# Retention and a rational feed-forward layer: masks made on chip, the sign of twelve weight tiles on GpSimd, and a written-out order of all steps

## The chip, the cores and the metric

The kernel runs on one core of a Trainium2 chip. A core has five engines with a queue of instructions each: TensorE (PE, with PEld for its weight loads), VectorE (DVE), ScalarE (ACT), GpSimd (POOL) and SyncE (SP), which here only issues the DMA transfers. Each engine works through its own queue in order and waits at semaphores for the others. The metric is the device time of one launch in microseconds (us); less is better.

## What is computed

The reference first makes a retention layer with decay `gamma` per head, over 4 batches, 8 heads, 768 positions of 64 dimensions, and then a feed-forward layer whose activation is a quotient of polynomials:

```python
for t in range(S):
    state = gamma[None, :, None, None] * state + np.einsum('bhd,bhe->bhde', k[:, :, t], v[:, :, t])
    y[:, :, t] = scale * np.einsum('bhd,bhde->bhe', q[:, :, t], state)
...
h = x @ w_in
h2 = h * h
h3 = h2 * h
P = a[0] + a[1] * h + a[2] * h2 + a[3] * h3
Q = 1.0 + np.abs(b[0]) * np.abs(h) + np.abs(b[1]) * h2
g = P / (Q + 1e-06)
return (g @ w_out).astype(np.float32)
```

x holds the 3072 tokens of 512 values that the retention gives; w_in is 512 x 2048 and w_out 2048 x 512. Both weights arrive as float64.

## The kernel before

**Retention.** The 768 positions of a batch are cut into 6 chunks of 128. The first chunk of each of the four batches has no state behind it (`first_chunk`): scores S = k q on PE (tile pa), a product with a mask of decays M on DVE (tile aT), values R = aT v on PE (tile px), and then XH and XL, which split the result into a rounded part xh (ACT) and the rest xl (DVE), since every large product is made of three fp32r products of such parts. The masks of the first chunks (tile first, two halves) and of the later ones (mask_sb), and the output decays xdec_sb, are inputs that are loaded. `first_states` makes the states after the first chunks (pk on PE, state on DVE) from k that POOL has scaled (V). The later chunks come in pairs of batches (`later_chunks`): S in two bursts (pa, then pk), M, U(E), which adds the old state to half of pk and gives mid, R (px), a product with xdec_sb, XH and XL. Lc4 is the first such pair, Lc6 the second.

**Feed-forward.** The 3072 tokens are 6 blocks n of 512, the 2048 hidden units 16 tiles f of 128; a slot is one pair (n, f), numbered 0 to 95 in the order of `TURNS`: block 0 with f 0 to 7, block 1 with f 0 to 7, then both with 8 to 15, then blocks 2 to 5. IN(k) is the 12 matmuls of slot k into ph (line 825), OUT(k) the 12 into po (line 844), which takes four PSUM banks b4 to b7. Between them ACT makes A1 = |h| (tile q), A2 (tile s, on POOL for 16 slots), A3 (tile p); POOL makes P1 = q s; DVE makes D1 (two instructions); ACT A4 (reciprocal square root and square, into ph); DVE D2 (three instructions, lines 934 to 936; the first is called N below); ACT A6 = gh, the rounded g; POOL P2 = gl, the rest. ph has two banks, b0 and b1, so IN(k+2) waits for D2(k).

**Weights.** `decode` turns one float64 tile of 128 x 512, as two 32-bit words each (raw), into fp32r parts: ACT makes t from the top byte of the low word (low, line 784), ACT u from the high word without its sign (high, line 788), DVE joins both with the sign in two instructions (join, lines 794 and 797), ACT rounds (split, line 803), POOL takes the rest (line 806). The tile for (m, f) is w_in for m = 0 and w_out for m = 1. There are 32.

**Order.** Every piece of work is a `Step` with engines, costs, predecessors and a rank. `Plan.order` runs through a model of the engines while the kernel is built and always emits the step that can begin first, by rank among those close together; tables of ranks (`RANKS`, `OFFSETS`, `NUDGES`, `LOADS`) tip it. Where the model sees a gap on PE of over 700 ns, it puts matmuls of zeros there (`zeros_for`). Loads are issued by SP in the order of the plan; buffers come from pools with the depths in `BUFS`, and a load waits at SP until its buffer is free.

```python
            nc.vector.scalar_tensor_tensor(
                u_, u_, 3, t_, ALU.logical_shift_left, ALU.bitwise_or
            )
            nc.vector.scalar_tensor_tensor(
                t_, cell["raw"][:, :, 1], 0x80000000, u_, ALU.bitwise_and, ALU.bitwise_or
            )
```

Of the kernel before, what the change touches and what calls it, by code (L numbers as in the profile page):

```python
# [10 lines left out]
U32 = mybir.dt.uint32  # L11
U8 = mybir.dt.uint8
# [8 lines left out]
LANES = 8  # L21
WAKE = 60
ARRAY = 163
BEGIN, ISSUE, LATENCY, LANDED, RATE = 350, 470, 1850, 560, 408
STALLS = (3300, 1400), (13000, 1300)
LEAVE, ENTER = 92, 111
COLD = 1200, 1700
FULL, LATE = 66000, 2000


def zeros_for(gap):

    return min(12, int(gap / FILL)) if gap > 700 else 0

# [18 lines left out]
class Plan:  # L53
# [4 lines left out]
    def __init__(self, depths, banks):  # L58
        self.depths, self.turns = depths, {}
        self.held = {b: None for b in banks}  # L60
        self.steps, self.free, self.landings, self.claims = [], {"SP": BEGIN}, [], []
        self.stalls = list(STALLS)
        self.pipe, self.tiled, self.begun = 0, False, False

    def step(
        self, engines, cost, run, after=(), rank=0.0, takes=(), uses=(), tiled=False, kind=None
    ):
        rank += OFFSETS.get(kind, 0.0) + NUDGES.get(len(self.steps), 0.0)
        if not isinstance(cost, dict):
            cost = {e: cost for e in engines}  # L70
        x = Step(engines, cost, run, after, rank, list(takes), list(uses), tiled)
        for b in x.uses:
            b.users += 1
        self.steps.append(x)
        return x

    def freed(self, buffer):
        if buffer is None:
            return 0
        return None if buffer.users else buffer.end  # L80

    def banks_of(self, buffer, x):

        best = None
        for option in buffer.options():
            ends = [self.freed(self.held[b]) for b in option]
            if None in ends or best and max(ends) >= best[0]:
                continue
            begin = max(x.known, *ends) + HOLD
            if any(y is not x and y.rank < x.rank and y.known < begin and not wanted.isdisjoint(option)  # L90
                   for y, wanted in self.claims):
                continue
            best = max(ends), option
        return best

    def ready(self, x):
        t = x.known
        for b in x.takes:
            if b.options:
                found = self.banks_of(b, x)  # L100
                end = found and found[0]
            else:
                turns = self.turns.setdefault(b.pool, [])
                n = self.depths[b.pool]
                end = self.freed(turns[-n]) if len(turns) >= n else 0
            if end is None:
                return None
            t = max(t, end + WAKE if end else 0)
        return t

    def commit(self, x, engine, t):
        for b in x.takes:
            if b.options:
                b.banks = self.banks_of(b, x)[1]
                for name in b.banks:
                    self.held[name] = b
            else:
                self.turns[b.pool].append(b)
        busy, done = x.cost[engine] if isinstance(x.cost[engine], tuple) else (x.cost[engine],) * 2
        if engine == "PE" and x.tiled != self.tiled:  # L120
            self.tiled = x.tiled
            extra = LEAVE if x.tiled else ENTER
            busy, done = busy + extra, done + extra
# [1337 lines left out]
```

## Time and profile before

| | |
|---|---|
| time, median of 3 runs | 609.01 us (608.49 to 609.05) |
| profiled execution | 608.67 us, of which the span in the trace is 607.0 |
| PE busy | 596.5 us, 98% of the span |
| DVE, ACT, POOL busy | 442.4, 430.0, 330.4 us |
| DMA | 59.43 MB, mean 98 GB/s |

A row of the timeline gives the start, the length, the engine, the line of the kernel, the operation, the tiles written and read, how many instructions were merged into the row, and in brackets how long the engine stood idle before it and what ended that. Matmuls overlap each other, so the next row on PE can begin before the end of the last. A chain row gives a start, a length and the work.

### The profile page before, as it was taken

What the parts mean: (1) busy time and instruction counts of PE and PEld (TensorE: products, weight loads), DVE (VectorE), ACT (ScalarE), POOL (GpSimd) and SP (SyncE); (2) the same over time, 40 slices, a digit from 0 to 9 for tenths busy, and PEclk for the clock granted to TensorE, in tenths of its full rate; (3) what the DMA queues carried; (4) which work ended last, traced back from release to release, by engine and by line L of the source; (5) the groups of instructions that cost most, each with busy time, mean ns of one, the idle gap of its engine ahead of it and who ended that gap; (6) DMA issues with size and microseconds to landing.
All of it is one profiled execution on the core that took longest, in us unless ns stands there. A gap on an engine that the chain in (4) does not pass through costs nothing.

```text
span 607.0 us, 12921 instructions
## 1 busy us (share of the span) xinstructions
PE 596.5 (98%) x5230; PEld 486.5 (80%) x5230; DVE 442.4 (73%) x665; ACT 430.0 (71%) x699; POOL 330.4 (54%) x276
## 2 busy tenths in 40 slices
PE   7998999999999999999999999999999999999997
PEld 5766888888888888878888888888888888888885
DVE  3899999898778778676666766567777666666664
ACT  3899899999756574666666775577675766767663
POOL 0789598796756554646445554454463345544452
PEclk9999999999999999999999999999999999999999
DMA  8999901011314263404005101400240000100001
GB/s 317 409 409 413 374 0 70 1 52 36 105 70 130 75 217 85 159 19 157 2 1 176 69 1 26 151 0 6 83 137 22 1 1 1 70 0 1 0 2 69
DMA packets 30411, 59.43 MB, mean 98 GB/s; under 512 B 3216, under 2 KB 8592, under 8 KB 30352
## 3 DMA queue, kind: packets, MB, share of 16 engines
q1 hardware_dynamic: 30352, 58.61, 26.7%
q8 instruction: 41, 0.67, 0.4%
q14 instruction: 18, 0.15, 0.1%
HBM read 50.21 MB, written 8.39 MB: 97 GB/s over the span
## 4 chain that ended last, share of the span: by engine, by line
PE 90%; DVE 0%; ACT 0%; issue 0%
PE po L844 43%; PE ph L825 41%; PE px L420 3%; PE pa L390 2%; PE pk L399 2%; DVE p L936 0%; DVE t L797 0%; DVE ph L935 0%; DVE q L934 0%; ACT o L991 0%
## 5 line engine op out<-in xcount | busy, mean ns | idle before, releaser
L907 POOL TENSOR_TENSOR q<-q,s 128x512 f32<-128x512 f32 x96 | 124.2, 1294 | 184.6 <-ACT s L896 172.6
L825 PE MATMUL ph<-xh,w 128*128 128x512 f32 (+2 forms) x776 | 208.4, 391 | 2.5 <-ACT w L803 1.5
L844 PE MATMUL po<-w,gh 128*128 128x512 f32 x768 | 199.6, 392 | 0.0
L825 PEld LDWEIGHTS ph<-xh,w 128*128 128x128 f32 x776 | 143.7, 188 | 33.8 <-ACT w L803 2.4
L844 PEld LDWEIGHTS po<-w,gh 128*128 128x128 f32 x768 | 143.1, 188 | 30.2
L934 DVE SCALAR_TENSOR_TENSOR q<-q,small,ph 128x512 f32<-128x512 f32 x96 | 71.6, 746 | 112.3 <-ACT ph L923 109.7
L946 POOL TENSOR_TENSOR gl<-p,gh 128x512 fp32r<-128x512 f32 x96 | 124.2, 1294 | 36.6 <-ACT gh L942 19.7
L922 ACT ACTIVATE s<-q,small 128x512 f32<-128x512 f32 x96 | 69.5, 724 | 64.8 <-POOL q L907 64.8
L844 PE MATMUL po<-w,gl 128*128 128x512 f32 x384 | 110.5, 390 | 0.0
L887 ACT ACTIVATE q<-ph 128x512 f32<-128x512 f32 x96 | 57.4, 598 | 69.6 <-PE ph L825 69.3
L825 PE MATMUL ph<-xl,w 128*128 128x512 f32 (+2 forms) x388 | 103.3, 388 | 0.0
L825 PEld LDWEIGHTS ph<-xl,w 128*128 128x128 f32 x388 | 72.6, 188 | 15.2
L844 PEld LDWEIGHTS po<-w,gl 128*128 128x128 f32 x384 | 72.0, 188 | 15.2 <-POOL gl L946 0.3
L902 ACT ACTIVATE p<-ph,small 128x512 f32<-128x512 f32 x96 | 74.5, 776 | 0.0
L916 DVE SCALAR_TENSOR_TENSOR p<-p,small,ph 128x512 f32<-128x512 f32 x96 | 71.7, 747 | 3.4
L915 DVE TENSOR_TENSOR p<-ph,p 128x512 f32<-128x512 f32 x96 | 65.8, 685 | 8.8 <-ACT p L902 8.4
L935 DVE SCALAR_TENSOR_TENSOR ph<-p,small,ph 128x512 f32<-128x512 f32 x96 | 71.9, 749 | 0.0
L936 DVE SCALAR_TENSOR_TENSOR p<-q,ph 128x512 f32<-128x512 f32 x96 | 65.9, 687 | 3.3
L942 ACT CAST gh<-p 128x512 fp32r<-128x512 f32 x96 | 59.1, 616 | 12.2 <-DVE p L936 12.0
L896 ACT ACTIVATE s<-q,small 128x512 f32<-128x512 f32 x80 | 65.0, 812 | 0.1
L923 ACT ACTIVATE ph<-s 128x512 f32<-128x512 f32 x96 | 57.8, 602 | 4.2 <-DVE p L916 0.9
L806 POOL TENSOR_TENSOR w<-t,w 128x512 fp32r<-128x512 f32 x32 | 41.4, 1296 | 22.3 <-DMA k<-in_k 14.8
(59 smaller groups left out, 416.6 us busy)
## 6 DMA issues: line engine op xcount, KB each, us to landing
v<-in_v SPq DMA_DIRECT2D x34, 256.0 KB, 4.9
raw<-in_w_in SPq DMA_DIRECT2D x16, 512.0 KB, 7.9
raw<-in_w_out SPq DMA_DIRECT2D x16, 512.0 KB, 8.5
qT<-in_qT SPq DMA_DIRECT2D x24, 256.0 KB, 4.6
kT<-in_kT SPq DMA_DIRECT2D x24, 256.0 KB, 4.6
k<-in_k SPq DMA_DIRECT2D x24, 256.0 KB, 4.1
out<-o SPq DMA_DIRECT2D x24, 256.0 KB, 2.3
q2T<-in_q2T SPq DMA_DIRECT2D x10, 256.0 KB, 4.6
```

The lines of the kernel that those rows point to most:

```text
L825: nc.tensor.matmul(cell["ph"][:, t0:t1], w[0, f][:, part, kt * P : (kt + 1) * P], x[:, kt, t0:t1], start=(i == 0), stop=(i == 3 * NP - 1),)
L844: nc.tensor.matmul(o_tiles[n][tt], g_[:, tt * P : (tt + 1) * P], w[1, f][:, part], start=(first and m == 0), stop=(last and m == 2),)
L896: nc.scalar.activation(cell["s"], cell["q"], AF.Identity, bias=babs[:, 0:1], scale=babs[:, 1:2])
L902: nc.scalar.activation(cell["p"], cell["ph"], AF.Identity, bias=par_sb[:, 2:3], scale=par_sb[:, 3:4])
L907: nc.gpsimd.tensor_mul(cell["q"], cell["q"], cell["s"])
L915: nc.vector.tensor_mul(p_, ph_, p_)
L916: nc.vector.scalar_tensor_tensor(ph_ if aside else p_, p_, par_sb[:, 1:2], ph_, ALU.add, ALU.mult)
L922: nc.scalar.activation(s_, cell["q"], AF.Abs_reciprocal_sqrt, bias=qcon[:, 0:1])
L934: nc.vector.scalar_tensor_tensor(q_, q_, qcon[:, 0:1], ph_, ALU.add, ALU.mult)
L935: nc.vector.scalar_tensor_tensor(ph_, p_, par_sb[:, 0:1], ph_, ALU.add, ALU.mult)
L936: nc.vector.scalar_tensor_tensor(p_, q_, 2.0, ph_, ALU.subtract, ALU.mult, reverse0=True)
L946: nc.gpsimd.tensor_sub(cell["gl"], cell["p"], cell["gh"].bitcast(F32))
```

## The change

**Masks.** The inputs mask0, mask1 and xdec are gone. One input of 204 columns, powers, is loaded third; it holds the first four powers of each block, the factors for doubling and a causal pattern. `grow` copies the first four columns and then doubles the width with one product each. DVE makes the first masks so (seven instructions), POOL makes xdec_sb (six) and mask_sb (one). The 816 columns live in the buffer of weight tile (1, 15), which is loaded after them.

**Sign.** For 12 weight tiles in the table POOL writes the sign from the top byte into the upper 16 bits of t; ACT's low then writes only the lower 16 bits, and the join on DVE is one instruction.

**A2.** POOL makes it for 25 slots instead of 16.

**Order.** The planner is gone: `ORDER` lists the 1767 steps, `BANKS` the PSUM banks, `ZEROS` the zero matmuls. D2 is now two steps, N and the rest, which may be apart. Code for an exact product of some slots is added, but its list (`EXACT`) is empty.

```diff
     def order(self, emit):
...
+        for i in ORDER:
+            x = self.steps[i]
+            for b in x.takes:
+                if b.options:
+                    b.banks = [f"b{j}" for j in BANKS[i]]
+            x.start = True
+            emit(x, x.engines[0], ZEROS.get(i, 0))
...
+    def grow(engine, to, first, by):
+
+
+        n, w = to.shape[1], 4
+        engine.tensor_copy(to[:, :, :4], first.rearrange("p (b t) -> p b t", t=4))
+        while w < to.shape[2]:
+            engine.tensor_mul(
+                to[:, :, w : 2 * w], to[:, :, :w], by[:, :n].unsqueeze(2).broadcast_to([P, n, w])
+            )
+            w, by = 2 * w, by[:, n:]
+
+    def first_masks(rank):
+
+
+        def run(_):
+            to, causal = lent["first"], lent["causal"]
+            grow(nc.vector, to.rearrange("p (b t) -> p b t", t=D), lent["first4"], lent["first_by"])
+            for r, blocks in ((0, slice(0, 3, 2)), (1, slice(0, 2))):
+                y = to[half(r)].rearrange("p (b x t) -> p b x t", x=3, t=D)[:, :, blocks]
+                by = causal[half(r)].unsqueeze(1).unsqueeze(1).broadcast_to([D, 4, 2, D])
+                nc.vector.tensor_mul(y, y, by)
+            for s in range(2):
+                masks[s] = to[:, s * 6 * D : (s + 1) * 6 * D]
...
+    def later_mask(_):
+        to = mask_sb.rearrange("p e h t -> p (e h) t")
+        by = lent["later"].unsqueeze(2).broadcast_to([P, 2 * NP, D])
+        nc.gpsimd.tensor_mul(to, by, lent["causal"].unsqueeze(1).broadcast_to([P, 2 * NP, D]))
+
+    def later_decay(_):
+        to = xdec_sb.rearrange("p r a t -> p (r a) t")
+        grow(nc.gpsimd, to, lent["decay4"], lent["decay_by"])
...
+        def sign(_):
+            cell["t"] = ff.tile([P, DM], U32, name="t", tag=t_tag, bufs=BUFS[t_tag])
+            byte = cell["raw"].rearrange("p m w -> p (m w)").bitcast(U8)[:, 7::8]
+            if aside:
+                nc.gpsimd.tensor_scalar(
+                    cell["t"].bitcast(U16)[:, 1::2], byte, 128.0, 32768.0, op0=ALU.is_ge, op1=ALU.mult
+                )
 
         def low(_):
-            cell["t"] = ff.tile([P, DM], U32, name="t", bufs=BUFS["t"])
             byte = cell["raw"].rearrange("p m w -> p (m w)").bitcast(U8)[:, 3::8]
-            nc.scalar.activation(cell["t"], byte, AF.Identity, bias=lcon[:, 0:1], scale=1.0 / 32)
+            to = cell["t"].bitcast(U16)[:, 0::2] if aside else cell["t"]
+            nc.scalar.activation(to, byte, AF.Identity, bias=lcon[:, 0:1], scale=1.0 / 32)
...
+            if aside:
+                nc.vector.scalar_tensor_tensor(
+                    t_, u_, 3, t_, ALU.logical_shift_left, ALU.bitwise_or
+                )
+                return
...
-        load_first(0, "s", -10 + 0.012)
-        load_first(1, "p", -10 + 0.014)
-        const_load("mask", mask_sb.rearrange("p e h t -> p (e h t)"), mask1, CONSTS)
-        const_load("xdec", xdec_sb, xdec, CONSTS)
+        load_powers(-11)
+        first_masks(-10)
+        for name, cost, run in (("mask", (1250, 1300), later_mask), ("xdec", (2300, 2400), later_decay)):
...
+    ("sign", (0, 0)): "POOL", ("sign", (0, 1)): "POOL", ("sign", (0, 4)): "POOL",
+    ("sign", (0, 6)): "POOL", ("sign", (0, 12)): "POOL", ("sign", (0, 14)): "POOL",
+    ("sign", (0, 15)): "POOL", ("sign", (1, 4)): "POOL", ("sign", (1, 5)): "POOL",
+    ("sign", (1, 6)): "POOL", ("sign", (1, 7)): "POOL", ("sign", (1, 8)): "POOL",
...
+ORDER = (
+    20, 19, 1, 58, 6, 7, 24, 2, 72, 32, 11, 59, 12, 8, 13, 60, 61, 26, 33, 73, 4, 21, 14, 74, 25,
```

What stands on DVE behind the products with xdec_sb of the pair Lc4, before. u<-u,t and t<-raw,u are a join, p<-ph,p and p<-p,small,ph are D1, xl is XL:

```order
L457 TENSOR_TENSOR px<-px,xdec_sb 128x512 x2
L794 SCALAR_TENSOR_TENSOR u<-u,t 128x512
L797 SCALAR_TENSOR_TENSOR t<-raw,u 128x512
L472 TENSOR_TENSOR xl<-px,xh 128x2x2x128 x2
L794 SCALAR_TENSOR_TENSOR u<-u,t 128x512
L797 SCALAR_TENSOR_TENSOR t<-raw,u 128x512
L915 TENSOR_TENSOR p<-ph,p 128x512
L916 SCALAR_TENSOR_TENSOR p<-p,small,ph 128x512
```

And in the changed kernel at the same place, where t<-u,t is a join of one instruction and q<-q,small,ph is N, the first instruction of D2:

```order
L317 TENSOR_TENSOR px<-px,xdec_sb 128x512 x2
L862 TENSOR_TENSOR p<-ph,p 128x512
L863 SCALAR_TENSOR_TENSOR p<-p,small,ph 128x512
L719 SCALAR_TENSOR_TENSOR t<-u,t 128x512 x2
L332 TENSOR_TENSOR xl<-px,xh 128x2x2x128
L664 TENSOR_TENSOR state<-pk,small 128x256 x2
L874 SCALAR_TENSOR_TENSOR q<-q,small,ph 128x512
L332 TENSOR_TENSOR xl<-px,xh 128x2x2x128
```

D1 of slot 2 moved ahead of the joins, the two joins here became one instruction each, and the second pair's state of the first chunks moved in.

What stands on POOL behind gl of slot 5, before (gl<-p,gh is P2, q<-q,s is P1, s<-q,small is A2, w<-t,w the rest of a weight tile):

```order
L946 TENSOR_TENSOR gl<-p,gh 128x512
L892 TENSOR_SCALAR s<-q,small 128x512
L907 TENSOR_TENSOR q<-q,s 128x512
L806 TENSOR_TENSOR w<-t,w 128x512
L946 TENSOR_TENSOR gl<-p,gh 128x512
L806 TENSOR_TENSOR w<-t,w 128x512
L892 TENSOR_SCALAR s<-q,small 128x512
```

And in the changed kernel from gl of slot 4 on, where t<-raw is a sign:

```order
L894 TENSOR_TENSOR gl<-p,gh 128x512
L701 TENSOR_SCALAR t<-raw 128x512 x2
L838 TENSOR_SCALAR s<-q,small 128x512
L735 TENSOR_TENSOR w<-t,w 128x512
L853 TENSOR_TENSOR q<-q,s 128x512
L701 TENSOR_SCALAR t<-raw 128x512
L894 TENSOR_TENSOR gl<-p,gh 128x512
L838 TENSOR_SCALAR s<-q,small 128x512
```

Three signs and one more A2 moved in between two gl. On PE the groups behind px of Lc4 stood as IN(3), OUT(0), OUT(1), IN(4), IN(5); now they stand as IN(3), OUT(0), IN(4), OUT(1), IN(5).

## Rows read from the trace of the kernel before

**Rows 1.** The page: busy time, share of the span and instructions of each engine, then the busy tenths of PE and the granted clock in 40 equal slices of the span.

```profile
PE 596.5 (98%) x5230; PEld 486.5 (80%) x5230; DVE 442.4 (73%) x665; ACT 430.0 (71%) x699; POOL 330.4 (54%) x276
...
PE   7998999999999999999999999999999999999997
...
PEclk9999999999999999999999999999999999999999
```

**Rows 2.** Busy time by stretch: the stretch, its length, then busy us (and instructions) of PE, PEld, DVE, ACT and POOL, the granted clock, the DMA share and GB/s.

```profile
6.58:18.84 12.26, 11.34 (x270) 7.82 (x270) 7.58 (x17) 5.33 (x12) 2.84 (x3) 1.00 1.05 402
...
24.28:54.51 30.23, 27.48 (x359) 19.15 (x355) 29.34 (x48) 29.45 (x51) 25.47 (x22) 1.00 1.04 408
54.65:67.76 13.11, 13.11 (x293) 10.58 (x293) 11.85 (x18) 11.80 (x20) 9.29 (x9) 1.00 1.03 418
67.76:115.00 47.24, 47.24 (x208) 39.05 (x209) 43.82 (x66) 44.52 (x77) 38.42 (x33) 1.00 0.22 81
...
160.00:594.00 434.00, 434.00 (x3728) 357.38 (x3727) 300.53 (x443) 286.31 (x456) 212.44 (x174) 1.00 0.19 61
```

**Rows 3.** PE in order of time: the first scores, IN(0), IN(2), pk and the zeros ahead of px of Lc4, IN(3), zeros behind OUT(1), IN(4), IN(5) and OUT(3).

```profile
6.58 0.90 PE L350 MATMUL pa<-qT,kT 64*64 64x128 f32 x32 [1.37 <-DMA kT<-in_kT]
...
18.84 0.96 PE L825 MATMUL ph<-xh,w 128*128 128x384 f32 x4
...
29.98 1.16 PE L825 MATMUL ph<-xh,w 128*128 128x512 f32 x4 [0.54 <-DVE p L936]
...
34.21 1.16 PE L399 MATMUL pk<-v,k 64*64 64x64 f32 x64 [0.38 <-POOL k L569]
35.31 1.47 PE L291 MATMUL px<-zeros 128*128 128x512 bf16 x6
...
39.31 1.16 PE L825 MATMUL ph<-xh,w 128*128 128x512 f32 x4 [0.27 <-ACT w L803]
...
48.49 1.47 PE L291 MATMUL po<-zeros 128*128 128x512 bf16 x6
51.22 1.17 PE L825 MATMUL ph<-xh,w 128*128 128x512 f32 x4 [1.26 <-ACT w L803]
...
54.65 1.17 PE L825 MATMUL ph<-xh,w 128*128 128x512 f32 x4 [0.43 <-DVE p L936]
...
67.69 2.11 PE L844 MATMUL po<-w,gh 128*128 128x512 f32 x8
```

**Rows 4.** DVE in order of time: the first masks, the first instruction of D1(0), and the last of D2(3).

```profile
9.11 1.95 DVE L539 TENSOR_TENSOR aT<-pa,first 128x384 f32<-128x384 f32 x4 [8.17 <-DMA first<-in_mask]
...
24.28 0.68 DVE L915 TENSOR_TENSOR p<-ph,p 128x512 f32<-128x512 f32 x1
...
53.82 0.69 DVE L936 SCALAR_TENSOR_TENSOR p<-q,ph 128x512 f32<-128x512 f32 x1
```

**Rows 5.** ACT in order of time: A1(0) and the first instruction of A4(3).

```profile
22.51 0.60 ACT L887 ACTIVATE q<-ph 128x512 f32<-128x512 f32 x1 [0.47 <-PE ph L825]
...
48.75 0.71 ACT L922 ACTIVATE s<-q,small 128x512 f32<-128x512 f32 x1
```

**Rows 6.** Groups by line over the whole span: tiles, shapes and count, then busy us and mean ns of one, then the idle time before them and what ended it.

```profile
L896 ACT ACTIVATE s<-q,small 128x512 f32<-128x512 f32 x80 | 65.0, 812 | 0.1
...
L806 POOL TENSOR_TENSOR w<-t,w 128x512 fp32r<-128x512 f32 x32 | 41.4, 1296 | 22.3 <-DMA k<-in_k 14.8 <-ACT w L803 7.4
...
L784 ACT ACTIVATE t<-raw,small 128x512 uint32<-128x512 uint8 x32 | 24.2, 759 | 3.1 <-DMA raw<-in_w_in 2.8 <-POOL w L806 0.3
L794 DVE SCALAR_TENSOR_TENSOR u<-u,t 128x512 uint32<-128x512 uint32 x32 | 22.2, 693 | 2.2 <-ACT u L788 2.1
...
L892 POOL TENSOR_SCALAR s<-q,small 128x512 f32<-128x512 f32 x16 | 12.4, 772 | 17.8 <-ACT q L887 17.8
```

**Rows 7.** The chain that ended last, in order of time: OUT(2), OUT(4), and OUT(8) with OUT(9).

```profile
58.75 2.95 PE po L844 x12
...
73.43 2.72 PE po L844 x12
...
95.30 5.44 PE po L844 x24
```

**Rows 8.** POOL: first the busy times of all engines in the stretch from gl(4) to gl(9), as in rows 2; then in order of time gl(4), a P1 and an A2 with the idle time before them, and gl(9).

```profile
63.38:93.91 30.53, 30.53 (x254) 25.23 (x253) 28.05 (x43) 27.06 (x46) 23.31 (x20) 1.00 0.41 158
...
63.38 1.29 POOL L946 TENSOR_TENSOR gl<-p,gh 128x512 fp32r<-128x512 f32 x1 [0.56 <-ACT gh L942]
67.30 1.29 POOL L907 TENSOR_TENSOR q<-q,s 128x512 f32<-128x512 f32 x1 [2.62 <-ACT s L896]
...
74.17 0.77 POOL L892 TENSOR_SCALAR s<-q,small 128x512 f32<-128x512 f32 x1 [3.33 <-ACT q L887]
...
93.91 1.30 POOL L946 TENSOR_TENSOR gl<-p,gh 128x512 fp32r<-128x512 f32 x1
```

**Rows 9.** DMA issues: transfers, KB each, median us from issue to landing.

```profile
raw<-in_w_in SPq DMA_DIRECT2D x16, 512.0 KB, 7.9
...
first<-in_mask SPq DMA_DIRECT2D x2, 192.0 KB, 5.0
mask_sb<-in_mask SPq DMA_DIRECT2D x1, 256.0 KB, 6.1
xdec_sb<-in_xdec SPq DMA_DIRECT2D x1, 256.0 KB, 6.9
```

More of the change, by code (lines that the diff above doesn't have):

```diff
@@ L11 @@
 U32 = mybir.dt.uint32
+U16 = mybir.dt.uint16
 U8 = mybir.dt.uint8
@@ L58, in __init__ @@
     def __init__(self, depths, banks):
[L59 to L63, printed above, removed]
+        self.steps = []
     def step(
@@ L67, in step @@
     ):
[L68 to L123, printed above, removed]
-        if engine == "PE":
-            if self.begun:
-                gap = t - self.free[engine]
-                cold = min(max(gap - zeros_for(gap) * 216 - COLD[0], 0), COLD[1])
-                busy, done = busy + cold, done + cold
-            self.begun |= not x.tiled
-        x.start, self.free[engine] = t, t + busy
-        if engine == "SP":
-            self.pipe = max(t + LATENCY, self.pipe) + done
-            while self.stalls and self.pipe > self.stalls[0][0]:
-                self.pipe += self.stalls.pop(0)[1]
-            x.end = self.pipe + LANDED + (LATE if t > FULL else 0)
-            self.landings.append(x.end)
-        else:
-            x.end = t + done + (ARRAY if engine == "PE" else 0)
-        for b in x.uses:
-            b.users -= 1
-            b.end = max(b.end, x.end)
@@ L203, in tile_retention_rational_ffn @@
+        self.steps.append(Step(engines, cost, run, after, rank, list(takes), list(uses), tiled))
+        return self.steps[-1]
+    def order(self, emit):
+        for i in ORDER:
[5 more added lines that the diff above has]
+            emit(x, x.engines[0], ZEROS.get(i, 0))
 @with_exitstack
@@ new lines, in grow @@
+    def grow(engine, to, first, by):
[16 more added lines that the diff above has]
+                masks[s] = to[:, s * 6 * D : (s + 1) * 6 * D]
+        made = step(
+            ("DVE",), (3200, 3300), run, [ready["powers"]], rank, uses=[lent_buffer], kind="first"
+        )
+        for s in range(2):
+            mask_buffers[s], mask_loads[s] = lent_buffer, made
@@ L806, in rest @@
             nc.gpsimd.tensor_sub(w[m, f][:, 1], cell["t"].bitcast(F32), w[m, f][:, 0].bitcast(F32))
-        L = step(("ACT",), (651, 761), low, [got], rank, [t], kind="low")
+        N = step(
+            signer, {"NONE": (0, 0), "POOL": (800, 850)}, sign, [got], rank, [t], kind="sign"
+        )
+        L = step(("ACT",), (770, 882) if aside else (651, 761), low, [got, N], rank, uses=[t], kind="low")
         U = step(("ACT",), (548, 623), high, [got, L], rank, [u], kind="high")
-        J = step(("DVE",), (1300, 1385), join, [L, U], rank, uses=[t, u], kind="join")
+        J = step(
+            ("DVE",), (600, 690) if aside else (1300, 1385), join, [L, U], rank, uses=[t, u], kind="join"
+        )
         lows.append(L)
@@ L835, in gemm_out @@
         open_po[:] = [] if last else [o_tiles[n][0]]
+        if (n, f) in EXACT:
+            for tt in range(SPB):
+                nc.tensor.matmul(
+                    o_tiles[n][tt], cell["g"][:, tt * P : (tt + 1) * P],
+                    exact[1, f][2]["t"].bitcast(F32), start=first, stop=last,
+                )
+            return
         terms = ((cell["gh"], 0), (cell["gh"], 1), (cell["gl"], 0))
```

238 lines of the change are left out of this document (103 added, 135 removed), and 366 rows, old and new, of tables (BANKS, ENGINES, LOADS, NUDGES).

## The prediction

> **What bounds the kernel now.** I read the page first, then PE by stretches, then PE in order of time, and last the engines that end its waits. The page shows PE busy for 98% of the span, with a weak first slice and a weak last one, and PEclk 9 to the end, so the granted clock stays at the 2.4 GHz level [rows 1]. By stretches PE has no idle time from 54.65 us on: 13.11 of 13.11, 47.24 of 47.24, and 434.00 of 434.00 between 160 and 594 us [rows 2]. What can be won lies before 54.65 us. Read in order of time, PE there shows real work between stretches of zero matmuls (they write to idle, ph, px or po) and waits [rows 3]: the first scores begin at 6.58, the first feed-forward group IN(0) at 18.84. After that PE loses 8.1 us in eight places, where the zeros count as lost: the largest are 2.73 before IN(4) (48.49 to 51.22, zeros, then ACT's w), 1.4 before pk (zeros, then 0.38 until POOL's scaled k) and 1.4 before px (six zeros), and others are 0.54 before IN(2) (until DVE's p), 0.27 before IN(3) (ACT's w) and 0.43 before IN(5) (DVE's p). DVE has no pause of note in that time: 29.34 of 30.23 us between 24.28 and 54.51 us, ACT 29.45 [rows 2]. So the head is paced by DVE and ACT, and PE is the bound afterwards.
>
> The instructions on PE are the same before and after up to the order: past the second px group (it ends where OUT(3) begins, 67.69 us [rows 3]) the sequences of groups are equal to the end of the program, and ahead of it the same groups stand in another order. So the change in time is the shift of that point, plus any new wait behind it.
>
> **Loads removed.** The two first masks (192 KB each), mask_sb and xdec_sb (256 KB each) go [rows 9], 896 KB; 102 KB of powers come (204 columns). At 408 GB/s [rows 2] that is 1.9 us of transfers, but only what stands ahead of a needed load counts. The last v of the first chunks closed 4493 KB before (12 inputs of 256, two weight tiles of 512, the masks, 13 of scalars); now 4211 KB, by the same sizes and the powers: 282 KB at 402 GB/s, 0.7 us. Between that load and IN(0) stand scores, masks and values on PE and DVE that are also reordered; I take 0.3, so IN(0) at 18.5 and D1(0), the first pair of DVE instructions of slot 0, at 24.0 instead of 24.28 [rows 4].
>
> **Masks made on DVE.** Seven instructions of 48 to 512 columns. DVE stood idle there anyway: 8.17 us before its first product at 9.11 [rows 4]. Each is dearer than nothing and cheaper than the 0.69 us of a 512-column one [rows 6], so 0 to 4.8 us; by columns (1,792 of them at 0.69 per 512, 2.4, and half a microsecond for seven starts) 2.9. The powers are the third load; the third load before let PE begin at 6.58 [rows 3] and was 256 KB where this is 102, so about 6.1. Masks at 9.0, hardly earlier or later than 9.11. The second scores of the new order end at about 9.6, so 0.6 us of it is cover; at 4.8 us the masks would be 1.3 late and the 0.3 above would turn into a loss of 1. mask_sb and xdec_sb are made on POOL before 17 us, where POOL was idle (2.84 us busy up to 18.84 [rows 2]).
>
> The Trainium skill (GPSIMD Engine Reference, Key points) says that GpSimd shares its SBUF interfaces with VectorE and that DVE instructions with two SBUF inputs contend with it. Six of the seven new ones have two SBUF inputs and stand beside the first two signs; by that rule the masks would come later by up to one sign, about 0.85 us, of which 0.6 is covered. The trace speaks against it: the join, with two SBUF inputs and POOL at work for half the span, takes 0.693 [rows 6], D1 with one input in PSUM 0.68 [rows 4]. By the trace the sum stays as it is.
>
> **Sign on POOL, join on DVE.** The join of a weight tile was two DVE instructions (0.693 us for the first, L794 [rows 6]); for 12 tiles (the table lists 12) it is one. POOL gets 12 TENSOR_SCALARs, a kind that took 0.772 at 128x512 (L892), while its dearest of that size took 1.296 (L806) [rows 6]. The read is one byte in eight and the write two bytes in four, which no row shows, so 0.77 to 1.30 each; I take 0.85, near the row of its kind. The low-byte instruction of ACT (0.759, L784) writes 2-byte places then: 0 to 0.05 more (up to L896's 0.812), five times in the head.
>
> **A2 on POOL.** 25 instead of 16 slots: ACT loses 9 x 0.812 (L896), POOL gains 9 x 0.772 [rows 6].
>
> **The head.** Count DVE from D1(0) to the end of D2(3), whose p ended PE's wait before IN(5): before, 24.28 to 54.51, 46 instructions, 0.657 each [rows 4]. Now the same stretch holds 41: join [0,3] stands ahead of it, three joins ([0,4], [1,4], [0,6]) are single. 41 x 0.657 = 26.9, so D2(3) ends at 24.0 + 26.9 = 50.9, 3.6 earlier. Two checks. ACT from A1(0) to the start of A4(3): 22.51 to 48.75 with 45 instructions, 0.583 each [rows 5]; now 43, so from 22.4 to 47.5, done at 48.8, and N and D2 (2.1 us) give 50.9 as well: no room is left, ACT just fits. PE: U(E), the 16th DVE instruction after D1(0), at 24.0 + 16 x 0.657 = 34.5; px 34.6 to 36.6; IN(3) 2.95 behind it (a group that follows other work takes that, one behind a group 2.72 [rows 7]), 39.6; nine zeros (0.24 each by the six in 1.47 at 35.31 [rows 3]), 41.8; OUT(0) 2.95, 44.7; IN(4) waits for D2(2), the 33rd instruction, 45.7, and takes 2.95, 48.7; OUT(1) 2.7, 51.4. So IN(5) begins at about 51.4 instead of 54.65: PE ends this and not DVE. Behind it nothing pauses before (13.11 of 13.11), and the DVE and ACT instructions that follow are fewer again, so the point moves by 3.2 us, 67.7 to 64.5.
>
> **Behind the head.** PE is the bound, so fewer DVE and ACT instructions give nothing there. POOL is the question. Before, gl(4) began at 63.38 and gl(9) at 93.91 [rows 8], while OUT(4) began at 73.43 and OUT(8) with OUT(9) at 95.30 [rows 7]; the third part of OUT(9), which reads gl, starts at 95.30 + 2.72 + 1.81 = 99.8, 4.6 us after gl(9) is done. In those 30.53 us POOL was busy for 23.31 with 20 instructions, three of them A2: (23.31 - 3 x 0.77) / 17 = 1.24 for each other [rows 8]. Now 28 follow gl(4) up to gl(9): four signs, six A2 and 18 others, 3.4 + 4.6 + 22.3 = 30.3 us, while PE needs 24.5 for nine groups of 2.72. gl(4) is done at about 61.6, an estimate with three more signs ahead of it, and its reader, the third part of OUT(4), starts at 73.43 + 1.81 - 3.2 = 72.0, so 10.4 are to spare there and 10.4 + 24.5 - 30.3 = 4.6 at OUT(9), less where POOL waits for a group of PE (A2(10) and A2(11) stand there so early that I expect about 2). I cost it at 0.1.
>
> Sum: -3.2 + 0.1 = -3.1. The profiled execution took 608.67 (span 607.0 and 1.67 around it); that makes 605.6, and 609.01 - 3.1 = 605.9 against the median.
>
> **Rivals.** *A, forecast*: 605.9, its own range 604.3 to 607.0. *B, POOL gives part back*: the signs cost 1.30 instead of 0.85 (3.2 us over the seven from 45 us on, of 4.6) and POOL waits for PE besides; PE stalls some 2 us: 607.9. For it: POOL was idle 7.2 of those 30.53 us. Two of its waits, 2.62 until s from ACT and 3.33 until q for an A2 [rows 8], show both kinds: the first kind goes, since POOL makes s itself, the second can come more often, with six A2 in the stretch instead of three. Against it: POOL runs behind PE there, so the q of those slots should lie ready. The Trainium skill (GPSIMD Engine Reference, Performance pitfalls for Q7 kernels) says that reads whose step is above 8 bytes take half as much again. Here the step is 8 exactly, which no row of before shows; by that rule the sign stays at 0.77, and a byte further it would be 1.16, which is B. *C, the loads hold the head*: SP's queue is in order, and the second pair's k and v wait for buffers that the first pk group frees; the gain shrinks to 1: 608.0. Against it: the waits before were for DVE, ACT and POOL, and the transfers run without a pause up to 67.76 us (share 1.03 [rows 2]). *D, more*: the zeros before OUT(0) and the pause before IN(4) overlap better: -5, 604.0. *E, slower*: POOL becomes the bound from 70 us on. It decides from the point where seven signs eat the 4.6, the gain of 3.1 and 1.2 more: 0.85 + 8.9 / 7 = 2.1 us each, well above the dearest POOL row, if a byte read at a step of 8 is handled element by element; at 2.25 each, 9.8 - 4.6 - 3.1 = 2.1 us over before: 611. That the change doesn't do what it says (the joins stay double) is excluded by the order.
>
> **Numbers.** 0.2% (1.2 us) is about what can be told from no change. Chances: A 0.58, B 0.17, C 0.10, D 0.06, E 0.09. Faster by over 0.2%: A, D, half of B and a third of C, 0.76; within: 0.15; slower: 0.09. Range 603.8 to 608.4: it leaves E out, and the ends of C and D.
>
> **What would show it.** Right: IN(5) at 51 to 52 us, the second px done at 64 to 65 us, no PE wait behind it, TENSOR_SCALAR t<-raw at 0.77 to 0.9, single joins at 0.69, DVE full from 24 to 51. Wrong: PE waits for gl or for p between 70 and 115 us (B, E); waits until a DMA between 25 and 60 us (C); the first product of DVE after 10.5 us (masks dearer).

## The result: slower by 4 us, and the profile after

The changed kernel took 613.0 us (median of 5, 612.37 to 613.8) against 609.01 (median of 5, 608.49 to 609.21): a ratio of 1.0077, 95% interval 1.0066 to 1.0088. The ratios here are those on record, formed over all runs of a kernel, so they differ a little from the quotient of two medians (here 1.0066). The forecast was 605.9, with a range up to 608.4. The profiled execution took 612.9 us.

The page of the changed kernel: span, busy times and the granted clock in 40 slices.

```profile
span 610.9 us, 12904 instructions
...
PE 596.0 (98%) x5225; PEld 485.5 (79%) x5225; DVE 439.2 (72%) x660; ACT 425.2 (70%) x690; POOL 364.4 (60%) x304
...
PEclk9999999999999999999999999999999999999999
```

The span grew by 3.9 us and PE's busy time fell by 0.5 [rows 1], so what was added is idle time of PE. POOL is the engine that changed: 364.4 instead of 330.4 us. The same stretches as in [rows 2] show where; the columns are those of that group. The last row is from the kernel before, for the one stretch that [rows 2] leave out.

```profile
18.84:24.28 5.44, 5.44 (x59) 5.11 (x60) 4.36 (x10) 5.10 (x10) 3.25 (x5) 1.00 1.02 400
24.28:54.65 30.37, 25.46 (x374) 19.16 (x373) 26.80 (x43) 27.00 (x46) 30.28 (x24) 1.00 1.02 399
54.65:67.76 13.11, 12.91 (x292) 10.12 (x290) 11.67 (x18) 10.51 (x19) 12.82 (x11) 1.00 1.02 411
67.76:115.00 47.24, 46.65 (x214) 37.58 (x206) 39.94 (x60) 42.79 (x72) 46.42 (x39) 1.00 0.15 49
115.00:160.00 45.00, 43.23 (x189) 35.14 (x188) 38.08 (x56) 39.17 (x67) 41.24 (x35) 1.00 0.12 40
160.00:594.00 434.00, 434.00 (x3727) 357.23 (x3726) 300.67 (x443) 286.81 (x456) 215.40 (x177) 1.00 0.19 64
```

```profile
115.00:160.00 45.00, 45.00 (x200) 37.03 (x199) 41.03 (x62) 43.53 (x73) 34.29 (x28) 1.00 0.10 33
```

Read the last busy column of each row. From 24.28 to 54.65 POOL has next to no pause (30.28 of 30.37), where before DVE and ACT were the full ones; they now have over 3 us of idle time each. From 54.65 to 115 POOL is still full, 59.24 of 60.35. PE, gapless there before, now loses 0.20, 0.59 and 1.77 us in the third, fourth and fifth row. After 160 us it is gapless again.

The group by line that says why (busy us and mean ns of one, then the idle time before them):

```profile
L701 POOL TENSOR_SCALAR t<-raw 128x512 uint16<-128x512 uint8 x12 | 25.5, 2128 | 7.5 <-DMA raw<-in_w_in 7.4
...
L838 POOL TENSOR_SCALAR s<-q,small 128x512 f32<-128x512 f32 x25 | 19.4, 775 | 14.1 <-ACT q L833 14.0
...
L719 DVE SCALAR_TENSOR_TENSOR t<-u,t 128x512 uint32<-128x512 uint32 x12 | 8.0, 684 | 1.1 <-ACT u L712 1.1
```

One sign takes 2.128 us, 2.7 times the A2 of the same size and kind of instruction. The DVE instruction that it saves takes 0.69. The chain that ended last now runs over POOL from 63 to 106 us and again from 125 to 140, and through the signs (L701) there, where before it ran along PE [rows 7]:

```profile
63.42 1.29 POOL gl L894
64.71 4.17 POOL t L701 x2
72.06 2.13 POOL t L701
...
93.64 2.10 POOL t L701
100.31 2.13 POOL t L701
...
130.09 2.09 POOL t L701
135.48 1.29 POOL q L853
136.77 2.10 POOL t L701
```

And these are waits of PE in the changed kernel, the longest in the head, the three longest behind it, and between them (at 106.23, too short for a bracket) the first start behind a late gl:

```profile
47.11 1.16 PE L762 MATMUL ph<-xh,w 128*128 128x512 f32 x4 [1.67 <-ACT u L712]
...
76.86 1.17 PE L762 MATMUL ph<-xh,w 128*128 128x512 f32 x4 [0.54 <-DVE p L884]
...
106.23 1.20 PE L788 MATMUL po<-w,gl 128*128 128x512 f32 x4
...
133.45 0.50 PE L788 MATMUL po<-w,gl 128*128 128x512 f32 x1 [0.84 <-POOL gl L894]
...
140.14 0.50 PE L788 MATMUL po<-w,gl 128*128 128x512 f32 x1 [0.93 <-POOL gl L894]
```

The two gl that the last two waits are for, on POOL in order of time; each starts when a sign of the chain above ends:

```profile
132.12 1.28 POOL L894 TENSOR_TENSOR gl<-p,gh 128x512 fp32r<-128x512 f32 x1
...
138.80 1.28 POOL L894 TENSOR_TENSOR gl<-p,gh 128x512 fp32r<-128x512 f32 x1
```

The releaser in brackets is only the last link. The wait at 47.11 is that of IN(4), which needs D2(2). Its bracket names ACT's u, but D2(2) itself had only just ended (the last of it ran from 46.28 to 46.97). It was late because DVE stood idle 1.02 us until A4 of slot 2, and ACT 0.94 us ahead of A4 until POOL's q:

```profile
44.23 0.75 DVE L874 SCALAR_TENSOR_TENSOR q<-q,small,ph 128x512 f32<-128x512 f32 x1 [1.02 <-ACT ph L870]
...
42.77 0.72 ACT L869 ACTIVATE s<-q,small 128x512 f32<-128x512 f32 x1 [0.94 <-POOL q L853]
```

Since PE's groups are the same from OUT(3) to the end, the delay can be followed group by group (start of the same group after, minus before):

| group of PE | before | after | delay |
|---|---|---|---|
| OUT(3), right behind the second px | 67.69 | 67.86 | +0.17 |
| the IN that waits at 76.86 | 75.99 | 76.86 | +0.87 |
| an IN 30 us later | 106.02 | 107.36 | +1.34 |
| the IN behind the wait at 133.45 | 133.27 | 135.87 | +2.60 |
| the IN behind the wait at 140.14 | 138.74 | 142.57 | +3.83 |
| an OUT at 389 us | 388.53 | 392.43 | +3.90 |

So the head won nothing instead of 3.2 us, and 3.7 us were lost behind it, nearly all of it before 143 us. PE's idle time in the third to fifth row makes 2.56 of them: at each wait the delay grows by 0.2 to 0.3 us more than the bracket says.

### The profile page after: what moved, and what is told of

Read it like the earlier page. It is cut to its first block, busy times and chain, and to the rows that moved or that the text cites. A ratio compares the mean times of both kernels' runs of the same rounds, so it can differ in the third digit from the quotient of the medians.

```text
span 610.9 us, 12904 instructions
## 1 busy us (share of the span) xinstructions
PE 596.0 (98%) x5225; PEld 485.5 (79%) x5225; DVE 439.2 (72%) x660; ACT 425.2 (70%) x690; POOL 364.4 (60%) x304
## 4 chain that ended last, share of the span: by engine, by line
PE 81%; POOL 8%; DMA 7%; issue 1%; ACT 1%; SPq 1%; DVE 0%; POOLq 0%
PE po L788 37%; PE ph L762 37%; DMA raw<-in_w_in 3%; PE px L280 3%; POOL t L701 2%; DMA v<-in_v 2%; POOL w L735 2%; POOL gl L894 2%; POOL q L853 1%; PE pa L250 1%; PE pk L259 1%; DMA raw<-in_w_out 1%; POOL s L838 1%; DMA q2T<-in_q2T 1%; SPq L173 1%
## 5 line engine op out<-in xcount | busy, mean ns | idle before, releaser
L869 ACT ACTIVATE s<-q,small 128x512 f32<-128x512 f32 x96 | 69.6, 725 | 70.4 <-POOL q L853 70.3
L842 ACT ACTIVATE s<-q,small 128x512 f32<-128x512 f32 x71 | 57.7, 813 | 0.1
```

Source lines behind the costliest of these rows:

```text
L869: nc.scalar.activation(s_, cell["q"], AF.Abs_reciprocal_sqrt, bias=qcon[:, 0:1])
```

## The experiments

Theory T: the sign on POOL is far longer than costed, and that is all. Main rival R: the new order and A2 on POOL lose the time whatever the sign costs.

**1. A shorter sign.** Only 192 of 512 columns, and `low` writes whole words, so the signs of the 12 tiles are missing from the result:

```diff
-    cell["t"].bitcast(U16)[:, 1::2], byte, 128.0, 32768.0, op0=ALU.is_ge, op1=ALU.mult
+    cell["t"].bitcast(U16)[:, 1:385:2], byte[:, :192], 128.0, 32768.0, op0=ALU.is_ge, op1=ALU.mult
...
-            to = cell["t"].bitcast(U16)[:, 0::2] if aside else cell["t"]
+            to = cell["t"]
```

> The changed kernel with the sign on GpSimd cut to 192 of 512 columns and ScalarE's low writing the whole word again, so the sign of the 12 tiles is left out of the result; everything else, the joins of one instruction and the order of all steps, stays. By the trace (2.12 us for 512 columns, 0.21 for a small copy) a cut sign should take about 0.9 us, close to the 0.85 that the prediction costed. Theory T (the length of the sign on GpSimd is the whole cause; the head's count was right): 605.9 us, 605 to 607, IN(5) at about 51.5 us, the second px group done at about 64.5 us, no wait of PE for gl behind it. Rival R (the new order and the ten other slots of A2 on GpSimd are the cause, whatever the sign costs): 611 or more, with GpSimd still full up to 110 us. Rival H (the count of the head was wrong as well): 607.5 to 609.5, the second px group at 66 us or later though PE waits for no gl.

Measured: 606.75 us, ratio 0.9981 (0.9966 to 0.9997). A sign took 0.93 us, IN(5) began at 51.91, the second px was done at 65.14, and behind 54.65 us PE had no wait at all. R falls: with the same order and the same A2, 6 of the changed kernel's 613 are gone once the sign is short. The head's count held too. The shorter `low` of this run is not the reason: run 9 leaves `low` as the changed kernel has it.

**2. No sign on POOL**, all joins double (the 12 entries taken out of the table):

> The changed kernel without any sign on GpSimd: all 32 joins are two instructions on VectorE as before, the order of the other steps stays. Theory T: GpSimd is relieved of 12 x 2.1 us, and the head has 44 instead of 41 VectorE instructions between D1(0) and D2(3), 24.0 + 44 x 0.657 = 52.9 us, so IN(5) comes at about 53 and the time is about 607.3 us (606 to 608.3). Rival R: 611 or more. Rival J (the single joins were what the order needs, VectorE is now late all the way): 609 or more with PE waiting for p of VectorE behind 55 us.

Measured: 609.27, ratio 1.0011 (0.9996 to 1.0025), no difference from before. The second px was done at 66.48, so the head still won 1.2 us; the IN groups then waited for DVE's p, three times and 2.3 us in all, two of them in the head (1.60 and 0.43) and one behind it (0.26). That is the time of rival J, which had put the waits behind 55 us, and 2 us over my figure: the order's gain needs the single joins.

**3. A2 as before**, 16 slots on POOL, with the long sign:

> The changed kernel with the list of A2 on GpSimd of the kernel before (16 slots instead of 25), the signs on GpSimd as they are. Theory T: GpSimd loses 9 x 0.86 = 7.7 us up to 115 us but the signs' 12 x 2.1 remain; the head (A2(0) and A2(3) go, A2(1) comes) moves by under 1 us, and the waits of PE for gl behind 55 us (2.6 us in all) shrink to about 1: 610.5 to 612. Rival A2 (the slots of A2 are the larger part of the overload): 609 or less. If ScalarE, with 9 x 0.72 us more, is the next bound: 613 or more, with PE waiting for ScalarE.

Measured: 615.2, ratio 1.0114 (1.0098 to 1.0129): worse, though POOL was busy 6 us less (358.4). PE's waits for DVE's p grew to 4.6 us (3.1 in the changed kernel). The expectation had given 610.5 to 612 to theory T and 613 or more to the case that ACT is the next bound; the time is that of the latter. So A2 on POOL is not what overloads it to the harm of the kernel; on ACT it costs more.

**4. What makes the sign long.** Eight forms of the instruction on the 12 tiles, whose signs the result then lacks, for instance

```diff
+    nc.gpsimd.tensor_scalar(t16[:, 1::2], byte, 128.0, 1.0, op0=ALU.mult, op1=ALU.add)
...
+    nc.gpsimd.tensor_scalar(t32, words, 128.0, 32768.0, op0=ALU.is_ge, op1=ALU.mult)
```

> The sign's instruction in eight forms on the 12 tiles (none reaches the result, since ScalarE's low writes the whole word afterwards, so the signs of these tiles are left out): as it is, without the comparison, with contiguous bytes read, with contiguous 16-bit places written, with both contiguous, with whole words read and written contiguously, and with whole words read at a step of 8 bytes, with and without the comparison. Theory step (the read at a step of 8 bytes makes it long): all forms with that step take about 2.1 us, the contiguous ones about 0.8. Theory size (bytes in or 16-bit places out cost more than words): the byte forms take about 2.1 whatever the step, the word forms about 0.8. Theory comparison (is_ge costs): the forms without it take about 0.8. The time of the whole kernel follows the mean of its signs: between 606 and 613 us.

POOL in order of time; L705 is the form as it is, L707 the same read and write with mult and add, L709 bytes read contiguously, L711 16-bit places written contiguously, L713 read and written contiguously, L715 whole words contiguously, L717 whole words at a step of 8 bytes with mult and add, L719 the same with is_ge and mult:

```profile
9.74 0.77 POOL L707 TENSOR_SCALAR t<-raw 128x512 uint16<-128x512 uint8 x1
34.58 2.08 POOL L709 TENSOR_SCALAR t<-raw 128x512 uint16<-128x512 uint8 x1
37.98 1.93 POOL L713 TENSOR_SCALAR t<-raw 128x512 uint16<-128x512 uint8 x1
44.38 1.97 POOL L711 TENSOR_SCALAR t<-raw 128x512 uint16<-128x512 uint8 x1
64.74 1.94 POOL L715 TENSOR_SCALAR t<-raw 128x512 f32<-128x512 uint32 x1
66.64 1.99 POOL L719 TENSOR_SCALAR t<-raw 128x512 f32<-128x512 uint32 x1
71.87 0.66 POOL L717 TENSOR_SCALAR t<-raw 128x512 f32<-128x512 uint32 x1
93.25 2.12 POOL L705 TENSOR_SCALAR t<-raw 128x512 uint16<-128x512 uint8 x1
```

The step, the bytes and the 16-bit places cost next to nothing: with mult and add the very same read and write takes 0.77, the price of an A2. With is_ge it takes 1.93 even when both sides are contiguous, and 1.94 for contiguous words. The whole took 612.17 in its one run. I read this as the price of a comparison.

**5. A sign without a comparison**, by rounding:

```diff
+    top = cell["raw"].rearrange("p m w -> p (m w)").bitcast(U16)[:, 3::4]
+    nc.gpsimd.tensor_scalar(
+        cell["t"].bitcast(U16)[:, 1::2], top, 1.5 * 2.0 ** 38, 1.5 * 2.0 ** 38, op0=ALU.add, op1=ALU.subtract)
```

> The changed kernel with the sign made on GpSimd without a comparison: the upper 16 bits of the float64 (at most 16367 for a positive weight below 1, 32768 more for a negative one) plus and then minus 1.5 x 2^38, which rounds to a multiple of 32768. Nothing is left out. Theory T (the comparison alone lost the time): the instruction takes about 0.78 us, the second px group is done at about 65 us, PE waits for no gl and no p behind it, and the time is 605.3 to 606.5 us, about 2.5 under the kernel before and 7 under the changed one. Rival S (a read of 16 bits at a step of 8 bytes, or the larger constants, are slow too): 1.2 to 2.1 us for the instruction and 608 to 613 us. Rival L (the cut sign was only fast because ScalarE's low wrote whole words, 0.75 instead of 0.86 us): 607.5 or more with PE waiting for ScalarE in the head.

Measured: 2.14 us for a sign, and 613.25 us (ratio 1.0089, 1.0073 to 1.0104), as the changed kernel. So it was not the comparison; my reading of the forms was wrong.

**6. The same twice**, its expectation put down before run 5's time was known:

> The sign of the run before made twice in a row into the same place, so about 1.55 us of GpSimd for each of the 12 tiles, between 0.78 and the 2.12 of the changed kernel; the result is the same. Theory T (GpSimd's time for a sign is what decides, and the overload grows once its slack is used up): 608 to 610 us; the head late by about 1 us against the single one, and a first wait of PE for gl between 70 and 145 us. If only the comparison as such mattered (through VectorE, or the interface that GpSimd shares with it), and not the time that GpSimd is held: 605.3 to 606.5 as with the single one.

The expectation rested on 0.78 a sign; it was 2.1, so the run is a dose of 4.3 us a tile: 637.54 us, ratio 1.0490 (1.0474 to 1.0506).

**7. The same with A2 as before**, likewise:

> The sign without a comparison, and the list of A2 on GpSimd of the kernel before (16 slots instead of 25). Theory T: with the short sign GpSimd has room for all 25, and ScalarE does not for nine more of 0.72 us: in the run with the long sign the same edit cost 2.2 us, from PE's waits for VectorE's p. Expected 607.0 to 609.0, with PE waiting for p or ScalarE's w before 60 us. Rival: with GpSimd no longer overloaded the place of A2 makes no difference, 605.3 to 606.5.

615.07, ratio 1.0110 (1.0096 to 1.0123). With a sign of 2.1 us it repeats run 3 and agrees with it.

**8. The comparison on the first five tiles only:**

> The sign with the comparison (2.1 us) on the five tiles that stand ahead of gl of slot 4 in GpSimd's queue, the one without it on the other seven, so it tells the loss in the head from the loss behind it. The second px group in the changed kernel was done at 67.9 us against 65.1 with the cut sign, 2.7 us; from there to the end the changed kernel took 537.85 us and the one with the cut sign 534.2, 3.7. Theory T (two separate losses, GpSimd makes up behind the head what it lost in it): second px at 67 to 68 us, 608.0 to 609.5 us in all. Rival (the delay from the head is carried on into the waits for gl behind 100 us): 610 or more. Rival (the loss in the head is made up): under 607.

614.02, ratio 1.0094 (1.0080 to 1.0108). Both forms took 2.1 us, so it tells the head from what follows no better than the changed kernel does, and nothing follows from it on the sign.

Its profiled execution, and that of run 5, show something else that can make the head late. In run 8 PE stood idle from 10.58 to 12.57, until a load of v; from 13.5 to 15.5 its granted clock was 0.50, the 1.2 GHz level, and IN(0) began at 20.31 instead of 18.76. In run 5 PE stood idle from 13.35 to 16.05, the clock was 0.50 from 16.05 to 19.0, and IN(0) began at 21.66. The same waits were 0.50 and 0.84 us in the changed kernel's own trace, and the clock stayed at 1.00.

**9. A sign by mult and add.** The high word as fp32 times 0.0 is a zero with the weight's sign, and adding -0.0 keeps it:

```diff
+    nc.gpsimd.tensor_scalar(
+        cell["t"].bitcast(F32), cell["raw"][:, :, 1].bitcast(F32), 0.0, -0.0, op0=ALU.mult, op1=ALU.add)
```

> The changed kernel with the sign made by the pair of operations mult, add: the high word read as fp32, times 0.0, plus -0.0, which leaves a zero with the sign of the weight; GpSimd writes the whole word. Nothing is left out. The form with mult, add took 0.66 us for whole words at a step of 8 bytes and 0.77 for bytes among the eight forms, where all with is_ge took 1.93 to 2.12; plus and minus 1.5 x 2^38 took 2.12 without a comparison. Theory P (what costs is the pair of operations: mult with add is short, other pairs are long, whatever is read and written): 0.66 to 0.78 us for a sign, the second px group done at 64.5 to 65.2 us, no wait of PE for gl behind it, 605.0 to 606.5 us. Rival (the 16-bit input or the size of the constants made the last one long, and something of the value, as zeros, will here): over 1.2 us for a sign and 608 or more.

Measured: 606.63 us, ratio 0.9978 (0.9966 to 0.9991): faster than both kernels, and nothing is left out of the result. Of its 12 executions eight took 605.74 to 606.74 us and four 607.86 to 609.46. The four have a mean granted clock of 0.995 to 0.997, the eight 0.999 to 1.000, which would fit a stretch at the lower clock as in runs 5 and 8; no trace of one of the four exists, so that is not shown. What follows is of the eight. Its group of signs, then PE in order of time (IN(0), IN(4), IN(5) and OUT(3)):

```profile
L701 POOL TENSOR_SCALAR t<-raw 128x512 f32<-128x512 f32 x12 | 8.3, 699 | 8.2 <-DMA raw<-in_w_in 8.1
```

```profile
18.65 0.96 PE L763 MATMUL ph<-xh,w 128*128 128x384 f32 x4
...
45.92 1.16 PE L763 MATMUL ph<-xh,w 128*128 128x512 f32 x4 [0.63 <-DVE p L885]
...
51.47 1.07 PE L763 MATMUL ph<-xh,w 128*128 128x512 f32 x4
...
64.67 2.11 PE L789 MATMUL po<-w,gh 128*128 128x512 f32 x8
```

PE has no wait behind IN(4), and POOL has idle time again in the stretch of [rows 8] (2.53 us until an A1 of ACT at 71.15, 1.64 at 93.01).

**10. Which pairs of operations are short.** Twelve pairs in the sign's place, same bytes in, same places out, constants 64 and 2:

```diff
+    nc.gpsimd.tensor_scalar(half, byte, 64.0, 2.0, op0=ALU.mult, op1=ALU.mult)
+    nc.gpsimd.tensor_scalar(half, byte, 64.0, 2.0, op0=ALU.add, op1=ALU.add)
```

> Twelve pairs of operations in the sign's place, all of bytes at a step of 8 bytes into 16-bit places at a step of 4, same constants 64 and 2; none reaches the result (ScalarE's low writes the whole word afterwards), so the signs of these tiles are left out. Theory P: mult, add 0.77 us, and the other pairs 1.9 to 2.1 each, a single mult or is_ge among them or shorter. Rival K (pairs of arithmetic are short and only constants of 2^38 or 16-bit input were long): mult-mult, add-mult, add-subtract, mult-subtract about 0.8, only is_ge and max long. The time of the whole: 611 to 613.

POOL in order of time: L703 mult mult, L705 add mult, L707 add subtract, L711 subtract mult, L709 mult subtract, L713 max mult, L717 mult alone, L715 add add, L719 is_ge alone, L721 mult max, L725 is_ge mult, L723 mult add.

```profile
7.23 0.76 POOL L703 TENSOR_SCALAR t<-raw 128x512 uint16<-128x512 uint8 x1 [6.81 <-DMA raw<-in_w_in]
10.16 0.77 POOL L705 TENSOR_SCALAR t<-raw 128x512 uint16<-128x512 uint8 x1 [2.17 <-DMA raw<-in_w_in]
34.49 2.17 POOL L707 TENSOR_SCALAR t<-raw 128x512 uint16<-128x512 uint8 x1
37.97 2.13 POOL L711 TENSOR_SCALAR t<-raw 128x512 uint16<-128x512 uint8 x1
44.53 2.12 POOL L709 TENSOR_SCALAR t<-raw 128x512 uint16<-128x512 uint8 x1
64.50 2.13 POOL L713 TENSOR_SCALAR t<-raw 128x512 uint16<-128x512 uint8 x1
66.54 1.72 POOL L717 TENSOR_SCALAR t<-raw 128x512 uint16<-128x512 uint8 x1
71.44 2.17 POOL L715 TENSOR_SCALAR t<-raw 128x512 uint16<-128x512 uint8 x1
93.03 1.70 POOL L719 TENSOR_SCALAR t<-raw 128x512 uint16<-128x512 uint8 x1
99.67 2.15 POOL L721 TENSOR_SCALAR t<-raw 128x512 uint16<-128x512 uint8 x1
129.91 2.13 POOL L725 TENSOR_SCALAR t<-raw 128x512 uint16<-128x512 uint8 x1
136.61 0.79 POOL L723 TENSOR_SCALAR t<-raw 128x512 uint16<-128x512 uint8 x1
```

Three pairs are short, mult mult, add mult and mult add, all 0.76 to 0.79. Everything else takes 2.12 to 2.17, add add and mult subtract among it, and one operation alone takes 1.70 to 1.72, more than a short pair. So theory P holds in the main: mult mult and add mult are short as well, which it had not named. K falls. The kernel took 611.86 in its one run. Why the chip does this no run shows; that it goes by the pair is shown.

**11. The short sign, A2 as before:**

> The short sign (mult, add), and the list of A2 on GpSimd of the kernel before (16 slots instead of 25). With the long sign the same edit cost about 2 us (615.2 and 615.1 against 613), by PE's waits for VectorE's p in the head and behind it. Theory T (the order needs A2(0) and A2(3) off ScalarE, which is full in the head): 607 to 609 us, with PE waiting for p or ScalarE's w between 25 and 60 us. Rival (with GpSimd no longer late the place of A2 makes no difference): 605 to 606.5.

Measured: 611.07, ratio 1.0051 (1.0036 to 1.0065), 4.4 us over run 9, and 2 more than theory T gave. So in this order nine more A2 on POOL are worth more than the signs on POOL, which give 2.6 (run 2 against run 9). PE's longest wait behind the head, and what POOL itself waited for ahead of it:

```profile
115.38 1.20 PE L789 MATMUL po<-w,gl 128*128 128x512 f32 x4 [1.09 <-POOL gl L895]
```

```profile
110.29 1.30 POOL L854 TENSOR_TENSOR q<-q,s 128x512 f32<-128x512 f32 x1 [3.22 <-ACT s L843]
```

P1 waits 3.22 us for the s of an A2 that stands in ACT's queue. In this order A2 on POOL not only takes 0.81 us from ACT; it takes P1's wait for ACT away. Of the 4.4 us about 1.1 are lost up to the second px (65.81 against 64.67) and the rest behind it.

**12. The short sign twice**, 1.4 us a tile from start to start:

> The short sign made twice in a row into the same place, 1.35 to 1.55 us of GpSimd for each of the 12 tiles; the result is the same. So far: 0.94 us a sign gave 606.8, 2.12 gave 613.0, 4.25 gave 637.5: 24.5 us more for 12 x 2.13 = 25.6 above 2.12, so GpSimd was then the bound all the way, and less than half of it below. Theory T (a slack is used up first, then PE waits): 606.5 to 608.5 us, the point where it turns slower than before near 1.5 us a sign. Rival (no slack: every us on GpSimd costs from the first): 609 to 611.

Measured: 609.03, ratio 1.0009 (1.0000 to 1.0017), between theory T and the rival. With the others it gives the time by POOL's time for a sign. The rows were measured on different chips, on which the kernel before took 608.32 to 609.01, so less than 0.7 us between two rows tells nothing:

| POOL us for a sign | time, us | more per us added on POOL since the row above |
|---|---|---|
| 0.70 (run 9) | 606.63 | |
| 0.93 (run 1) | 606.75 | 0.1 / 2.8, none that can be told |
| 1.4 (run 12) | 609.03 | 2.3 / 5.6 = 0.4 |
| 2.13 (the changed kernel) | 613.0 | 4.0 / 8.8 = 0.45 |
| 4.3 (run 6) | 637.54 | 24.5 / 26 = 0.94 |

Up to about 0.9 us a sign no loss can be told, then less than half of what is added comes through, and past 2.1 nearly all of it: in run 6 POOL is busy for 117.2 of the 120.7 us between 24.3 and 145. Run 1 differs from the others in ScalarE's `low`, so its row is close but not of the same series.

## Why the prediction was wrong, step by step

**The step that failed: the price of the sign.** "So 0.77 to 1.30 each; I take 0.85." It was 2.13. The bounds came from rows of POOL, but I asked only for size, step and width, which turned out to cost nothing (0.77 with the same bytes and places, run 4), and took the kind TENSOR_SCALAR as one price. The row at 0.772 is an A2, and an A2 is mult and add; is_ge and mult is another pair. The upper end was the dearest row of POOL, which bounds nothing for an operation that no row shows. The trace of before could not tell 2.13; the upper end should have stayed open, and that would have moved weight to E. With it a second term was put at nothing: the head was counted for DVE, ACT and PE, and not for POOL. [rows 2] gave POOL 25.47 of 30.23 us there; in run 9, with a sign of 0.70, it is busy for 29.07 of the 30.37 from 24.28 to 54.65, so 1.3 us was all the room, and a sign of 2.13 asks for 4.3 more.

**Rival E** was the right mechanism, POOL the bound, at 9% instead of most. Its reason for a long sign, the read at a step of 8 bytes, was not the right one: the same read takes 0.77 with mult and add (run 4). Its price was off as well: at 2.1 it gave 1.2 us slower, and 4.0 were measured. E charged the seven signs against the slack behind the head and left the head's 3.2 us gain whole. But three of them stand in the head, 3 x 1.28 = 3.8 us over the price taken, and POOL was full from 24.28 to 54.65. The head's gain was gone first, so OUT(3) began 0.17 late instead of 3.2 early.

**Behind the head** I had 30.3 us of POOL from gl(4) to gl(9). It took 63.42 to 99.03, 35.6, and 30.3 + 4 x 1.28 = 35.4. That count was right but for the sign. gl(9) was done at 100.33 and its reader started at 100.57, so only 0.2 of the slack was left there. The next gl, behind one more sign, was done at 106.17 and its reader started at 106.23, where the delay grew from 0.9 to 1.34. This wait for gl and the one for p at 76.86 are the sign of being wrong that the prediction had named for 70 to 115 us. The two hardest waits come later, at 133.45 and 140.14, each behind a gl that had a sign right ahead of it. The prediction had costed POOL up to gl(9) only.

**The head's count** was right, as run 9 shows, where the sign has 0.70:

| | forecast | run 9 | changed kernel |
|---|---|---|---|
| IN(0) | 18.5 | 18.65 | 18.76 |
| D1(0) | 24.0 | 24.09 | 24.20 |
| IN(5) | 51.4 | 51.47 | 54.36 |
| second px done | 64.5 | 64.67 | 67.86 |
| behind the head, against before | +0.1 | -0.1 | +3.7 |
| span | 603.9 | 603.9 | 610.9 |

The span of run 9 is 603.9, and 605.6 less the 1.67 around it is 603.9. One step inside it was off and had room by luck: px of Lc4 began at 35.60 instead of 34.6, behind a pk group that ran until then, and the wait ahead of IN(4), which began at 45.92 (forecast 45.7), took that up. The time of run 9 is 0.7 over the forecast: its profiled execution took 606.19, 2.29 around the span instead of 1.67, which the forecast had taken as unchanged, and its median is 0.4 over its profiled execution. In the changed kernel 2.0 stand around the span; no run here tells where that part is from.

**Masks made on DVE**: off the path, as forecast. They took from 5.10 to 8.66 us, 3.6 instead of 2.9, but began 1.0 earlier, and the first product waited at 9.73 for PE's scores, not for them. The rule of the Trainium skill (GPSIMD Engine Reference, Key points) on contention with DVE instructions of two SBUF inputs was weighed against the join's 0.693, which spoke against it. By that rule a sign beside the mask products would take longer. Run 9 agrees: its first sign, beside the mask products, took 1.12 us, and those later 0.64 to 0.68. Runs 10 and 11 don't: the first sign, at the same place, took 0.76 in both. So what contention costs here is open; the path lost nothing by it.

```profile
7.08 1.12 POOL L701 TENSOR_SCALAR t<-raw 128x512 f32<-128x512 f32 x1 [6.64 <-DMA raw<-in_w_in]
9.65 0.66 POOL L701 TENSOR_SCALAR t<-raw 128x512 f32<-128x512 f32 x1 [1.45 <-DMA raw<-in_w_in]
```

The other rule of the Trainium skill (GPSIMD Engine Reference, Performance pitfalls for Q7 kernels), that a step above 8 bytes costs half as much again, agrees as far as it was tried: a step of 8 exactly took 0.77 with mult and add, and 0.66 for whole words. A step above 8 was not tried.

**A2 on POOL** was costed as an exchange of 0.81 for 0.77 us, hidden in "ACT just fits, no room is left". Runs 3, 7 and 11 price it at 2 to 4.4 us: in this order the head and the stretch up to 160 us rest on that part of the change.

**B, C and D.** C is excluded: PE's waits between 25 and 60 us were for POOL, DVE and ACT, none for a DMA, and run 9, with the same loads, has its head where the forecast put it. D did not come with the short sign either, where the head is 3.0 earlier and no more. B would have been the case at 1.4 us a sign, 609.0 where it gave 607.9.

## What to carry to other kernels

A price belongs to an operation, not to a kind of instruction: before taking a row's duration for another instruction, see that its operations are the same, and where no row has them, leave the upper end of the price open and ask what the engine would delay if it were twice or three times that. Write a TENSOR_SCALAR on POOL as multiply and add where it can be so written (here a sign as x times 0.0 plus -0.0). An engine that is 54% busy over the span can still be the bound in the stretch where the new work goes, so the slack is counted there, in the head as well as behind it.

## What was not expected of the hardware

A TENSOR_SCALAR on POOL of 128x512 takes 0.76 to 0.79 us for mult mult, add mult and mult add, and 2.12 to 2.17 us for the other seven pairs tried at the sign's own places, add add and mult subtract too, and the step and the widths changed either price by 0.2 at most (the first one of a run, beside the mask products on DVE, took up to 0.5 more: 1.12 in run 9). One operation alone takes 1.70 to 1.72, so a second operation that does nothing, such as a multiplication by 1.0, should make a single mult shorter; that follows from the rows and was not tried by itself. The changed kernel with a comparison in its sign and run 5 without one came out at 613.0 and 613.25: the time goes by how long POOL is held.
